# A gated delta rule followed by a softplus layer: another written-out order of the same operations

## The chip, the cores and the metric

The kernel runs on one core of a Trainium2 chip. The core has five engines that run side by side: TensorE (PE in the profile; its weight loads are PEld), VectorE (DVE), ScalarE (ACT), GpSimd (POOL) and SyncE (SP), which here only issues transfers. Each engine takes its own instructions strictly in the order in which the program lists them, and waits on semaphores for what the others produce. Transfers between the chip's memory and the core's run on 16 DMA engines. The metric is the device time of one execution in microseconds (us), lower is better.

## The reference

Two layers. The first is a recurrence over time with a 48 x 48 state for each of 4 x 8 pairs of batch and head, 768 steps long; the second works on its output, 3072 rows of 384.

```python
# q, k, v, g: (4, 8, 768, 48), beta: (4, 8, 768); all float32
k_n = k / (np.linalg.norm(k, axis=-1, keepdims=True) + 1e-06)
state = np.zeros((B, H, D, D))
for t in range(S):
    readout = np.einsum('bhd,bhde->bhe', q[:, :, t], state)
    y[:, :, t] = g[:, :, t] * readout
    v_old = np.einsum('bhde,bhd->bhe', state, kt)          # kt = k_n[:, :, t]
    state = state + bt * np.einsum('bhd,bhe->bhde', kt, vt - v_old)
x = y.transpose(0, 2, 1, 3).reshape(B * S, H * D)          # 3072 x 384
h = x @ w_in                                               # 384 x 2048
out = softplus(h) @ w_out                                  # 2048 x 384
```

## The kernel before

The recurrence is cut into 12 chunks of 64 steps (c = 0 to 11). Within a chunk the 64 dependent updates are replaced by products with the inverse of a triangular 64 x 64 matrix; only the state is carried from chunk to chunk. All 32 pairs of batch and head are worked on together.

For each chunk, `norms` squares k (ksq), sums (red) and takes roots (sqrt for the first four chunks, pow on GpSimd for the rest). `front` scales or casts k and q to 16 bits (kmul, cast), transposes them on TensorE (trs), evicts the transposes to the tile kqt (kev, qev), and forms the products of keys with keys and of keys with queries (gramk, gramq, gram), whose evictions are kkc and mask. `inverse`, once for each pair of chunks, inverts the blocks of 16 of the triangular matrices in place, lane by lane: diag and prep, then 15 steps (step c.0 to c.14, each a product and a sum on VectorE or GpSimd, each depending on the one before), then transposes back (st), and the matmuls xmm, tmm and zmm with their evictions (xs, td2, z) put the blocks together. `chain` carries the state: ks and qs are the products of keys and queries with the old state, w subtracts from v, umm and zu apply the inverse (evictions u1 and u2), smm and s make the new state, ymm and y the output of the chunk, and ytr with xt turn it around for the second layer. `vs 1` scales v of chunk 1 on GpSimd. `dense` is the second layer: g1 (x times w_in, into one of two PSUM buffers h), soft (softplus on ScalarE), g2 (times w_out, into the one PSUM buffer o), o (its eviction) and store. Groups of g1 and g2 are called `g1 chunk.block` and `g2 chunk.half.block`. `fill` groups are matmuls of the identity that nobody reads; 13 of the 40 defined are used.

Transfers: `load` brings half a tile of k, q, v or g (192 KB) and is issued by SyncE, as are the small beta loads (bload). `wload` brings a quarter of w_in (w0.0 to w0.3) or of w_out (w1.0 to w1.3), 384 KB each, and is issued by GpSimd, which also converts to 16 bits on the way. `store` writes 64 rows of the output (96 KB) and is issued by SyncE or ScalarE. An engine that reaches a transfer whose buffer is not free, or whose data is not made, waits there with everything behind it.

The order is written out: `_ORDER` is a string of words, a letter for the engine that is to do an operation (P TensorE, D VectorE, A ScalarE, G GpSimd, S SyncE) and the operation's number. `Program.emit` walks through the words and records each operation's instructions. So the words of one letter, read alone, are that engine's queue. How the words of different letters are interleaved decides only which buffer of a ring an operation gets, since a ring hands out the one that has been free longest. The rings that matter here: 12 buffers f for loaded tiles and squares, 5 PSUM buffers d for the recurrence, 2 for h, 1 for o, 16 for the output of softplus.

```python
    def emit(self, table):
        for word in table.split():
            en, no = word[0], int(word[1:])
            ...
            it.fn(en)
```

Lines of the profile that are spoken of: L305 and L302 are the loads, L330 the weight loads, L351 and L353 the squares on ScalarE and on GpSimd, L209 and L211 the copies on ScalarE and on VectorE or GpSimd (evictions among them), L454 and L422 the transposes of q and k, L516 gram, L656, L664 and L671 the steps of the inverse, L744, L768 and L789 xmm, tmm and zmm, L826 ks and qs, L842 vs 1, L866 w, L880 umm, L893 zu, L910 smm, L936 ymm, L963 ytr, L989 g1, L1001 softplus, L1016 g2, L1035 the stores, L1046 the fillers, L1056 the loading of ScalarE's softplus table.

## Time and profile before

| | us |
|---|---|
| three runs | 244.29, 249.46, 248.98 (median 248.98) |
| the profiled execution | 243.45 |
| its span, first to last instruction | 241.7 |
| mean granted clock of TensorE in it | 0.964 of full speed |

Busy time in the span: TensorE 219.1 us (91%), VectorE 164.8 (68%), ScalarE 154.7 (64%), GpSimd 108.4 (45%). The chain of work that ended last is 73% TensorE: 26% of the span at L1016 and 25% at L989, the two products of the second layer.

How rows are read: in an answer by stages, a row gives the stretch, its length, then for TensorE, its weight loads, VectorE, ScalarE and GpSimd the busy time with the number of instructions in brackets, then TensorE's granted clock, the mean busy share of the DMA engines and GB/s. In the order of time, a row gives the start, the duration, engine, line and operation, and in square brackets how long the engine had been idle and what ended that. In the groups, the figures behind the bar are the busy time of the group and the mean of one instruction in ns, and then the idle time ahead of them. Rows of transfers end with the size of one and the median time from issue to landing. Matmuls are pipelined: one's duration includes its way through the array, so that the durations of neighbours overlap.

### The profile page before, as it was taken

The numbers are of one execution on the slowest core, as the hardware profiler recorded it, in microseconds if no ns is written. First come the engines' busy times: TensorE is split into PE (matmuls) and PEld (weight loads), VectorE is DVE, ScalarE is ACT, GpSimd is POOL, SyncE is SP. The second block draws the span as 40 slices with busy tenths as digits, with TensorE's granted clock in tenths as the row PEclk, the third lists the DMA queues.
The fourth block names the chain that finished last, engine by engine and source line by source line (L and its number), as shares of the span: only waits on it lengthen the run. The fifth ranks groups of instructions, "written<-read, shape, count | busy, mean of one in ns | idle before, by whom it ended". The sixth has DMA issues, their size and how long they took to land.

```text
span 241.7 us, 11163 instructions
## 1 busy us (share of the span) xinstructions
PE 219.1 (91%) x4892; PEld 137.8 (57%) x4892; DVE 164.8 (68%) x378; ACT 154.7 (64%) x296; POOL 108.4 (45%) x180
## 2 busy tenths in 40 slices
PE   7695689886969999998999999999999999999993
PEld 2342377655756764565655566555666555677761
DVE  7898887877979887977799887997496150503000
ACT  6876755683865799896797635568763566253540
POOL 8151297767879468687399581313320000000000
PEclk9769956999999999999999999999999999999999
DMA  6999999999999388978699261922316100211122
GB/s 103 169 219 199 143 128 195 160 195 184 179 219 142 67 141 159 186 145 103 158 157 165 43 113 35 181 52 50 70 22 134 35 19 20 51 35 33 35 49 66
DMA packets 86833, 27.56 MB, mean 114 GB/s; under 512 B 77048, under 2 KB 86776, under 8 KB 86784
## 3 DMA queue, kind: packets, MB, share of 16 engines
q1 hardware_dynamic: 82064, 22.60, 54.7%
q0 software_dynamic: 3840, 3.17, 9.1%
q10 hardware_dynamic: 880, 1.08, 1.8%
q8 instruction: 38, 0.62, 1.2%
q14 instruction: 11, 0.09, 0.1%
HBM read 25.26 MB, written 4.72 MB: 124 GB/s over the span
## 4 chain that ended last, share of the span: by engine, by line
PE 73%; DMA 4%; ACT 3%; issue 2%; DVE 2%; POOL 1%; ACTq 0%; POOLq 0%
PE o L1016 26%; PE h L989 25%; DMA f<-in_g_dram 4%; PE d L936 3%; PE d L826 3%; PE d L516 2%; PE d L910 2%; PE d L893 2%; PE d L963 2%; PE d L454 1%; PE d L422 1%; PE d L768 1%; PE d L789 1%; PE d L744 1%; PE d L880 1%
## 5 line engine op out<-in xcount | busy, mean ns | idle before, releaser
L1016 PE MATMUL o<-w_out,ga 128*128 128x384 f16 x384 | 77.3, 327 | 0.6 <-ACT osb L209 0.6
L1001 ACT ACTIVATE ga<-h 128x512 f16<-128x512 f32 x96 | 56.6, 599 | 33.1 <-PE h L989 29.6
L989 PE MATMUL h<-xt,w_in 128*128 128x512 f16 (+1 forms) x384 | 73.6, 327 | 0.8 <-ACT xt L209 0.7
L989 PEld LDWEIGHTS <-w_in 128*128 128x128 f16 x384 | 35.0, 98 | 22.2 <-issue 1.5
L1016 PEld LDWEIGHTS <-ga 128*128 128x128 f16 x384 | 33.8, 98 | 20.8 <-issue 0.8
L664 POOL TENSOR_TENSOR tmp<-nn,tt 128x56 f32<-128x56 f32 (+7 forms) x47 | 16.8, 357 | 33.4 <-DVE tt L671 22.5
L373 POOL TENSOR_TENSOR nv<-nv,half_c 128x16 f32<-128x16 f32 x8 | 23.5, 2933 | 0.8 <-DVE nv L362 0.8
L209 ACT ACTIVATE u<-d 128x384 f16<-128x384 f32 x33 | 15.3, 491 | 9.6 <-PE d L893 5.2
L209 ACT ACTIVATE kqt<-d 128x1024 f16<-128x1024 f16 (+1 forms) x19 | 18.6, 977 | 4.2 <-PE d L454 2.2
L498 DVE TENSOR_TENSOR mt<-d,mask 128x256 f16<-128x256 f32 x48 | 18.4, 416 | 3.7 <-PE d L516 2.4
L671 POOL TENSOR_TENSOR tt<-tt,tmp 128x56 f32<-128x56 f32 (+7 forms) x47 | 17.3, 367 | 3.7
L1046 PE MATMUL h<-ident 128*128 128x512 f16 x52 | 17.2, 486 | 1.7 <-DVE ident L197 1.7
L209 ACT ACTIVATE osb<-o 128x384 f32<-128x384 f32 x20 | 9.8, 490 | 13.2 <-PE o L1016 13.0
L924 DVE TENSOR_TENSOR s<-s,d 128x384 f16<-128x384 f16 x20 | 10.3, 547 | 9.2 <-PE d L910 9.2
L406 POOL TENSOR_TENSOR kn<-f,nv 128x768 f16<-128x768 f32 x9 | 13.9, 1539 | 5.4 <-DVE nv L383 3.1
L211 DVE CAST u<-d 128x384 f16<-128x384 f32 x15 | 8.3, 556 | 9.9 <-PE d L893 7.6
L209 ACT ACTIVATE kk<-d 128x256 f16<-128x256 f32 x38 | 13.0, 386 | 2.1 <-DVE mt L498 0.8
L950 DVE TENSOR_TENSOR yg<-d,f 128x384 f16<-128x384 f32 x24 | 12.1, 547 | 3.1 <-PE d L936 1.9
L753 DVE TENSOR_TENSOR xs<-d,mk 128x256 f16<-128x256 f32 x24 | 9.2, 412 | 6.8 <-PE d L744 6.6
L664 DVE TENSOR_TENSOR tmp<-nn,tt 128x96 f32<-128x96 f32 (+7 forms) x37 | 9.7, 263 | 5.8 <-POOL tt L671 5.0
L866 DVE TENSOR_TENSOR w<-f,d 128x384 f16<-128x384 f32 x22 | 11.5, 547 | 3.0 <-POOL f L842 1.4
L516 PE MATMUL d<-kqt 48*64 48x128 f16 (+1 forms) x448 | 10.6, 220 | 2.3 <-issue 0.9
(114 smaller groups left out, 344.5 us busy)
## 6 DMA issues: line engine op xcount, KB each, us to landing
f<-in_k_dram SPq DMA_DIRECT2D x24, 192.0 KB, 5.8
f<-in_v_dram SPq DMA_DIRECT2D x24, 192.0 KB, 5.3
f<-in_q_dram SPq DMA_DIRECT2D x24, 192.0 KB, 5.4
f<-in_g_dram SPq DMA_DIRECT2D x24, 192.0 KB, 5.0
out_dram<-osb SPq DMA_DIRECT2D x37, 96.0 KB, 2.8
w_in<-in_moe_w_in_dram POOLq DMA_DIRECT2D x4, 384.0 KB, 6.3
w_out<-in_moe_w_out_dram POOLq DMA_DIRECT2D x4, 384.0 KB, 8.5
out_dram<-osb ACTq DMA_DIRECT2D x11, 96.0 KB, 2.4
```

What stands on the lines that cost most here:

```text
L209: nc.scalar.activation(o, x, AF.Copy, scale=float(sign))
L373: nc.gpsimd.tensor_tensor(nvs(), nvs(), half_c[:, :NU], ALU.pow)
L406: ENG[en].tensor_tensor(kn[c].ap[:, sl, :, :D], kf.ap[:, sl], nv.ap[:, :NU].rearrange("p (a h) -> p a h", a=2)[:, sl, :, None] .broadcast_ ...
L498: nc.vector.tensor_tensor(mt[c][m].ap[:, NP * p : NP * p + NP], gb[m].ap.rearrange("p (i b) -> p i b", i=NP)[:, :, n : n + C], mask[:, Non ...
L516: nc.tensor.matmul(gb[m].ap.rearrange("p (i b) -> p i b", i=NP)[HALF[r], i, lo:hi], x[:, :C], x[:, lo:hi],)
L664: ENG[en].tensor_tensor(t, nn.ap[:, :, j : j + 1, j + 1 :].broadcast_to([P, 2, w, n]), tt.ap[:, :, :w, j : j + 1].broadcast_to([P, 2, w, n ...
L671: ENG[en].tensor_tensor(rows, rows, t, ALU.add)
L950: lambda en, m=m: nc.vector.tensor_tensor(heads(yg.ap, m), hd(yp[m].ap), heads(gf.ap, m), ALU.mult),
L989: nc.tensor.matmul(hp.ap[:, n * b : n * b + n], w_in[:, j, f * P : (f + 1) * P], xt.ap[:, j, t0 : t0 + n], start=(j == 0), stop=(j == 2),)
L1001: lambda en, hp=hp, o=gb: nc.scalar.activation(o.ap, hp.ap, AF.Softplus),
L1016: nc.tensor.matmul(op.ap[:, :DM], b.ap[:, col + c0 : col + c0 + 128], w_out[:, f, :], start=(f == 0), stop=(f == NF - 1),)
L1046: nc.tensor.matmul(hp.ap, ident, ident[:, None, :].broadcast_to([P, 4, P]))
```

## The change

Only the string `_ORDER` is replaced. The operations are the same, with two fillers exchanged for two others, so there are 13 as before. On each engine the new queue is the old one with operations moved by some places, and 130 or so operations change their engine, mostly evictions between VectorE and ScalarE and steps of the inverse between VectorE and GpSimd. TensorE has 376 operations before and after, VectorE 325 and 329, ScalarE 302 and 308, GpSimd 110 and 104, SyncE 141 and 137. No group on TensorE moves by more than 13 places; on SyncE the first 20 transfers stay as they are. Nearly all buffers are handed out differently.

The diff, cut to a few of its lines:

```diff
@@ -1064,71 +1064,72 @@
 _ORDER = """
-S25 S26 S33 S34 S30 S60 S29 D9 D11 A8 D3 D5 D222 D176 D0 G198 P143 P144 S35 S59 P132 S36 D2 A1 A10
...
-G239 D192 D193 A270 D240 D243 D241 A242 A244 A288 D245 D246 P250 G248 A249 P259 G121 G123 G356 G122
...
-A1262 P1268 P1265 A1266 P1269 P1270 A1271 A1273 S1272 P1274 P1275 P1276 P1277 A1278 S1279 S1280
+S25 S26 P143 S33 D310 A7 D9 P132 S34 D11 A8 D3 D5 A1 D222 A10 S30 S60 D176 A169 P141 D0 D2 A173 G16
...
+A242 P296 D245 S32 P149 A270 A244 P250 D246 S31 A288 P259 S24 S17 D251 G248 A249 D252 P253 G123 D247
+S18 A254 G122 S22 A356 D398 D261 A255 S23 G121 D260 P188 A297 G125 D190 D189 P711 A713 A712 D289
...
+P1277 A1278 A1279 S1280
 """
```

Read by engine, with the operations' names, the parts that the prediction speaks of (before, then after):

```
TensorE, chunk 0
 - trs q2, fill 7, fill 35, xmm 0, xmm 1, tmm 0, umm 0, zmm 0, gramq 1.0, gramq 0.0, zu 0, trs q3, ymm 0, smm 0, fill 18, ytr 0, trs k3.0, g1 0.0
 + trs q2, trs q3, fill 20, xmm 0, xmm 1, tmm 0, gramq 0.0, umm 0, gramq 1.0, zmm 0, zu 0, smm 0, ymm 0, fill 18, ytr 0, trs k3.0, g1 0.0
ScalarE, chunk 0
 - ksq 3, tx 0.1, td2 0.1, td2 0.0, u1 0.1, sqrt 3, z 0.1, table, u2 0.1, s 0.0, qev q3, s 0.1, xt 0
 + ksq 3, tx 0.1, td2 0.0, ksq 4, td2 0.1, qev q3, u1 0.1, u1 0.0, sqrt 3, z 0.1, u2 0.1, table, s 0.0, xt 0, kev k3.0, s 0.1
GpSimd
 - tx 0.0, wload w0.0, wload w0.2, ksq 4, wload w0.1, wload w1.0, fix, clear 2, clear 4, wload w1.1, pad, kmul 2.0, pow 4, kmul 4.0, wload w0.3, vs 1, prep 2.0
 + tx 0.0, wload w0.2, wload w0.1, wload w0.0, wload w1.0, wload w1.1, diag 2, diag 4, kmul 2.0, pow 4, kmul 4.0, wload w0.3, vs 1, prep 2.0, prep 2.1
VectorE, chunk 1
 - ln 2, mask 2.00, pick 2, w 1.0, prep 2.1, w 1.1, red 5, step 2.2
 + ln 2, mask 2.11, pick 2, w 1.0, w 1.1, td2 1.1, mask 2.01, step 2.0, z 1.0, step 2.2
TensorE, chunk 1
 - zmm 1, umm 1, fill 4, g1 0.12, gramq 1.1, qs 1, zu 1, g2 0.1.4, ymm 1, gram 4.1, g1 0.14, ytr 1, smm 1
 + zmm 1, umm 1, gramq 1.1, g2 0.1.4, qs 1, fill 4, zu 1, g1 0.12, ymm 1, smm 1, g1 0.14, ytr 1, gram 4.1
Second inverse, engine of the steps 2.0 to 2.14
 - G G D D D G G D G D G G G G G
 + D G D D G G D D G D G D D G G
SyncE, from the 19th transfer
 - k4.0, bload, k3.0, k3.1, k4.1, bload, g0.1, k5.1, g0.0, 6 x bload, v1.0, v1.1, k5.0, g1.0, g1.1
 + k4.0, bload, k5.1, k3.0, k3.1, k4.1, bload, g0.1, g0.0, 6 x bload, v1.1, v1.0, g1.1, k5.0, g1.0
SyncE, about the 60th
 - q9.1, q7.0, q7.1, k9.0, v3.0, k9.1, v3.1, g3.1, g3.0, store 1.01, store 1.00, v5.0
 + q8.1, k11.1, g3.1, store 1.00, k9.0, v5.0
The last stores
 - ScalarE: o 11.0, store 11.01, o 11.1; SyncE: store 11.00, store 11.10, store 11.11
 + ScalarE: o 11.0, store 11.00, store 11.01, o 11.1, store 11.10; SyncE: store 11.11
```

More of the change, by code (lines that the diff above doesn't have):

```diff
@@ new lines @@
+A731 A732 P945 S46 D317 G318 P729 P133 D217 D377 P733 D218 S82 G319 D320 A735 S73 P933 A734 A934
+A930 P739 D321 P736 D740 G322 P935 D741 G128 P742 A383 D323 A936 D737 A743 P371 D373 D374 G324 D325
+A372 P951 A952 S74 P965 D326 D738 G327 D375 P366 P384 A367 P744 G328 S81 A966 A332 A368 D369 D331
+P946 G378 D745 D329 P959 A330 D333 S75 P953 S47 A960 P947 A385 D746 A954 G486 D334 A336 P957 G487
+A948 P338 P955 D370 G337 D339 S115 S76 D340 A444 P347 S84 P341 D335 A956 P937 A342 D343 D379 S91
+D349 G380 P748 S48 P344 P961 A464 A345 D346 D749 A750 P381 D445 G446 A451 P747 D348 P751 D382 A962
@@ new lines @@
+D752 P938 D465 G466 S54 S55 A753 P757 D759 S950 S53 P754 P939 S98 D755 P386 A387 A388 D447 G448 P940
+A941 D756 D758 S83 P391 A393 A392 D390 P963 D389 S99 A964 D395 A958 P762 D396 P967 P350 P968 A352
+A351 P760 S92 S114 D397 G400 A761 P969 D764 P449 D763 S56 P970 D401 D402 G403 G404 D450 P766 D768
+D767 A971 P353 S972 S97 P974 A355 A471 A354 G405 D467 S69 D394 P452 A453 P765 D406 D407 P975 P769
+A771 A770 P976 D408 D409 D410 P472 P775 D777 P772 A473 P977 D776 G468 A552 P778 D773 A539 S116 P454
```

113 lines of the change are left out of this document (51 added, 62 removed).

## The prediction

> **What bounds the kernel now.** I read the page first, for the slices of the span, then the busy time of each engine in stages, and last the start in order of time, engine by engine.
>
> ```profile
> span 241.7 us, 11163 instructions
> PE   7695689886969999998999999999999999999993
> PEclk9769956999999999999999999999999999999999
> DMA  6999999999999388978699261922316100211122
> ```
>
> The profiled execution took 243.45 us, so 1.75 us lie outside its span. A digit stands for 6.04 us. The DMA engines are at 9 from the second slice to the fourteenth (85 us), and TensorE is at 9 from the thirteenth (72 us) on, but for one 8 and the last slice. So there are two parts: a start that waits for data and for short dependent steps, and a plateau.
>
> ```profile
> 40.09:50.33 10.24, 8.99 (x219) 6.86 (x217) 7.86 (x18) 6.96 (x19) 8.23 (x8) 1.00 1.18 170
> 50.33:60.57 10.24, 7.72 (x271) 5.69 (x270) 7.99 (x22) 5.71 (x12) 7.21 (x18) 1.00 1.37 191
> 60.57:80.00 19.43, 17.43 (x495) 12.76 (x485) 17.20 (x35) 13.12 (x30) 15.94 (x17) 1.00 1.01 178
> 80.00:234.00 154.00, 152.84 (x3420) 93.53 (x3419) 98.28 (x218) 99.74 (x187) 56.96 (x104) 1.00 0.47 87
> ```
>
> The first number after each stretch is its length, the second TensorE's busy time. From 80 to 234 us it idles for 1.16 us of 154. The change issues the same 376 groups of matmuls, 13 of them fillers as before. So on the plateau an order can lose, but it can win at most 1.2 us. From 40.09 to 80 us TensorE idles for 39.91 - 8.99 - 7.72 - 17.43 = 5.8 us: this is all that better cover in the start can give back once dense work has begun.
>
> **The start, chunk 0.** Three things change around 28 to 40 us. ksq 4 moves from GpSimd to ScalarE, between the two evictions td2 0.0 and td2 0.1. The eviction qev q3 goes ahead of u1, and u1 0.0 goes from VectorE to ScalarE behind u1 0.1.
>
> ```profile
> 28.02 0.83 ACT L351 ACTIVATE f<-f 128x768 f32<-128x768 f32 x1
> 30.68 0.66 ACT L209 ACTIVATE td<-d 128x256 f16<-128x256 f32 x2 [0.78 <-PE d L768]
> 32.07 0.56 DVE L211 CAST u<-d 128x384 f16<-128x384 f32 x1
> 33.12 1.28 ACT L1056 ACT_TABLE_LOAD   x1
> 37.30 1.02 ACT L209 ACTIVATE kqt<-d 128x1024 f16<-128x1024 f16 x1
> 40.27 0.81 PE L989 MATMUL h<-xt,w_in 128*128 128x256 f16 x6
> ```
>
> On ScalarE a square costs 0.83 us, so td2 0.1 ends at 31.34 + 0.83 = 32.17 and umm 0 follows that late. Then qev q3 (1.02) and two u1 (0.88 together) stand in line: u1 is complete at about 34.1 instead of 32.07 + 0.56 = 32.6. Half of this comes back, because the table load (1.28, and 0.20 for its dummy) stood ahead of u2 0.1 and now stands behind it. With the new place of smm 0 ahead of ymm 0 I get xt 0 some 0.6 us later, and the first dense matmuls (g1 0.0) at 40.9 instead of 40.27.
>
> g1 0.0 also needs the first quarter of w_in, which was the first weight load and is now the third.
>
> ```profile
> 29.92 1.62 POOL L330 DMA_DIRECT2D w_in<-in_moe_w_in_dram  x2
> 33.03 0.80 POOL L330 DMA_DIRECT2D w_in<-in_moe_w_in_dram  x1
> w_in<-in_moe_w_in_dram POOLq DMA_DIRECT2D x1, 384.0 KB, 5.1
> w_in<-in_moe_w_in_dram POOLq DMA_DIRECT2D x1, 384.0 KB, 8.2
> ```
>
> The two landing times belong to the first load and to the third. The third is now issued at 29.92 + 1.62 = 31.54, so it lands between 36.6 and 39.7 us; I take the later, its own row. That is 1.2 us ahead of 40.9, so it is hidden; if chunk 0 came sooner, this load would be what is late next.
>
> Most of the 0.6 us is lost in idle time behind it, because chunk 1 has a gate of its own:
>
> ```profile
> 47.46 1.74 POOL L842 TENSOR_TENSOR f<-f,nv 128x768 f32<-128x768 f32 x1 [1.06 <-DMA f<-in_g_dram]
> f<-in_v_dram SPq DMA_DIRECT2D x2, 192.0 KB, 14.7
> 49.23 0.55 DVE L866 TENSOR_TENSOR w<-f,d 128x384 f16<-128x384 f32 x1 [1.35 <-POOL f L842]
> ```
>
> The scaling of v for chunk 1 waits for a load (the row names g; v 1 is what it reads, and v took 14.7 us to land, beside 1.9 MB of weights). All five early weight loads still stand ahead of it and the same bytes precede v 1 on SyncE, k5.1 included, so I leave 47.5 us where it is. I charge 0.2 us of the 0.6 (bounds 0 and 0.6). k5.1 ahead of k3 and k4.1 delays those by about one load; ksq 4, now earlier in ScalarE's queue, has td2 0.1 behind it and would pass the wait on.
>
> **Chunk 1 and the second inverse.** td2 1.1 moves from ScalarE to VectorE, behind w 1.1, which waits for that load.
>
> ```profile
> 48.80 0.64 ACT L209 ACTIVATE td<-d 128x256 f16<-128x256 f32 x2
> 50.70 0.43 PE L880 MATMUL d<-w,td 64*64 64x48 f16 x31 [0.68 <-DVE w L866]
> 50.32 0.24 POOL L656 TENSOR_TENSOR tt<-nn,tt 128x30 f32<-128x30 f32 x1 [0.43 <-DVE nn L644]
> 61.31 0.25 POOL L664 TENSOR_TENSOR tmp<-nn,tt 128x30 f32<-128x30 f32 x1
> L664 POOL TENSOR_TENSOR tmp<-nn,tt 128x56 f32<-128x56 f32 (+7 forms) x47 | 16.8, 357 | 33.4 <-DVE tt L671 22.5
> L664 DVE TENSOR_TENSOR tmp<-nn,tt 128x96 f32<-128x96 f32 (+7 forms) x37 | 9.7, 263 | 5.8 <-POOL tt L671 5.0
> ```
>
> The pair w 1 ends at 49.23 + 2 x 0.55 = 50.33, and an eviction of this size then takes some 0.4 us; zmm 1 queues behind that with 32 small matmuls (like umm's 0.43 us), and umm 1 behind zmm 1: I put it at 51.2 to 51.4, some 0.6 us later than the 50.70 above. smm 1 in turn now follows ymm 1 directly, so this is mostly returned before chunk 2.
>
> What chunk 2 waits for is the second inverse, 15 steps in a chain between GpSimd and VectorE, from 50.32 to the last product at 61.31 and its sum, about 61.9 us. Both prep 2 are now on GpSimd and step 2.0 on VectorE behind td2 1.1 and a mask: it starts about 0.8 us later. Three more of the 15 steps are net on VectorE (four go there, one goes back). A step is a product and a sum, on VectorE 0.09 us shorter each by the two means (their shapes differ somewhat), so 3 x 0.19 = 0.6 us is won; three more hand-overs cost an estimated 0.1 us each. Sum +0.5 us, bounds 0 and 1.5, as VectorE has other work between its steps. TensorE had 2.0 us idle from 60.57 to 80, so nothing covers this for certain: I charge 0.5 us.
>
> **The plateau and the end.** Loads and stores are shuffled on SyncE. The tightest place I found is k9.0, now behind store 1.00:
>
> ```profile
> 82.19 2.09 SPq L1035 DMA_DIRECT2D out_dram<-osb  x2
> f<-in_v_dram SPq DMA_DIRECT2D x1, 192.0 KB, 3.6
> 86.88 0.85 ACT L351 ACTIVATE f<-f 128x768 f32<-128x768 f32 x1
> ```
>
> Issued some 0.6 us behind that store, with the 3.6 us of a load just after, it lands at 86.4 us, 0.5 us before ksq 9 on ScalarE needs it. Hidden; if late, ScalarE holds softplus behind it and g1 runs out of its two buffers. Four more stores are issued by ScalarE, where it idles for a third of the plateau: nothing charged.
>
> At the end the last two stores of 64 rows, both on SyncE before, go one by ScalarE and one by SyncE.
>
> ```profile
> 238.09 1.11 SPq L1035 DMA_DIRECT2D out_dram<-osb  x2
> ```
>
> Half of these 1.11 us, 0.55, leaves the end. Sum: 0.2 + 0.5 - 0.55 = +0.15 us on 243.45, 243.6 us for an execution like the profiled one.
>
> **How that stands to the runs.** Three runs took 244.29, 248.98 and 249.46 us, the profiled one 243.45: two groups, 5 us apart, and the middle of the three is in the upper. The profile shows only a lower one. I forecast the centre of what was seen, (243.45 + 244.29 + 248.98 + 249.46)/4 = 246.55, plus 0.15: **246.7 us**, within 1.3% of either group.
>
> **The clock.** What differs between executions may be TensorE's clock:
>
> ```profile
> L1046 PE MATMUL h<-ident 128*128 128x512 f16 x2 | 0.6, 378 | 0.0
> 21.12 1.03 PE L1046 MATMUL h<-ident 128*128 128x512 f16 x4
> 24.39 0.61 PE L454 MATMUL d<-ident,qn 128*128 128x128 f16 x8
> 5.96:9.37 3.41, 1.66 (x43) 0.88 (x41) 2.27 (x6) 2.51 (x6) 0.73 (x3) 1.00 1.40 157
> 16.20:19.61 3.41, 1.44 (x14) 0.70 (x12) 3.01 (x12) 2.46 (x3) 0.00 (x0) 1.00 1.08 233
> 26.44:29.85 3.41, 1.19 (x68) 0.81 (x66) 2.58 (x5) 2.99 (x6) 0.48 (x1) 1.00 1.20 174
> 29.85:33.27 3.41, 2.25 (x111) 2.05 (x112) 3.33 (x7) 1.83 (x7) 3.34 (x5) 0.50 0.55 67
> 33.27:36.68 3.41, 3.21 (x118) 3.01 (x118) 2.03 (x7) 1.72 (x3) 3.41 (x6) 0.50 1.24 190
> 36.68:40.09 3.41, 3.41 (x29) 2.19 (x22) 3.25 (x8) 2.48 (x4) 2.20 (x3) 0.50 1.24 199
> ```
>
> In the last six rows the figure before the last two (1.00 or 0.50) is the granted clock, constant over each 3.41 us. It fell to half after stretches with 1.66 and 1.19 us of TensorE work, and came back only after one full of large matmuls. The Trainium skill, "TensorE: Matmul & The Clock Gate", Part 1, says that this window is free-running, that one idle window halves the clock and one busy window restores it. By that rule alone the clock would have come back at 36.68, after a window 94% busy, and chunk 0 would have ended up to 1.7 us sooner; the trace has 0.50 until 40.09, and the row decides.
>
> **Rivals.** First, the start stays warm. trs q3 and a filler now stand right before xmm 0, inside 26.44:29.85. By the first three rows this stretch had 0.6 us of large matmuls (half a filler) and gets a filler (1.03) and eight transposes (0.61), about 1.5 with their overlap; 16.20:19.61 kept its clock with 1.44. Then the 8.87 us of work in the three half-clock rows shrink by up to 4.4 us. On chunk 0's path I count at most half of that, and w_in (39.7 us) and v 1 (47.5) cap it: 1 to 2 us, so 241.6 to 242.6 for the profiled kind; and if the upper group comes from the clock, the middle run drops to the lower one, 242.5 to 243.5. For it: the place of the fillers. Against: the margin is next to nothing. Chance 0.30.
>
> Second, on the other side: the clock comes back late. In 36.68:40.09 it was the filler, ytr 0 and trs k3 that filled the window; chunk 0 now comes 0.6 us later and its small matmuls move into that window. If one that starts later must release it, dense work begins at half clock: each further window costs 1.7 us of TensorE time, three of them 5.1. It decides once that work exceeds the 2.5 us idle between 50.33 and 60.57. The profiled kind would take 248.6 us, and the middle run 248.98 + 5.1 = 254.1. For it: 33.27:36.68, busy and not released. Against: w_in lands in time. Chance 0.25.
>
> **How the numbers follow.** The forecast has the remaining 0.45. Two per cent (5 us) is about what these runs can tell from no change: below 244.0 is faster, above 254.0 slower. The warm case gives faster nearly always, 0.28, and the forecast's lower group touches 244.0: 0.04 more, 0.32 in all. The late case gives slower where all three windows are lost, 0.16 of its 0.25, with 0.04 for stalls on the plateau that I missed: 0.20. The rest, 0.48, is no change. The range goes from 242.0, inside the warm case, to 254.2, past the late case's 254.1; below and above it I leave 0.08 and 0.10.
>
> **What would show it.** In the profile after: PEclk in the slices from 30 to 40 us (warm or not); g1's first row near 40.9 us; the scaling at L842 near 47.5; the last step of the second inverse near 62.4; one store on each queue at the end, 0.5 us sooner. I am wrong if waits of TensorE over 1 us show after 80 us, if L842 has moved by more than 2 us, or if clock digits below 9 stand after 45 us.

## The result, and the profile after

Sixteen executions of the changed kernel have a median of 245.85 us (244.06 to 247.38), sixteen of the kernel before 244.72 us (242.11 to 249.46). The ratio is **1.0078, 95% interval 1.0053 to 1.0104**: slower by 0.8%, 1.9 us, less than the 2% that I called no change, but more than the measurement's own uncertainty. The ratio leaves out executions over 1.5% above the fastest of their kernel, which the old order has here and the new one has not; the medians of all executions are only 0.5% apart, their means 0.2%. The profiled execution took 246.25 us (before 243.45).

The page of the changed kernel, the same rows as before (a digit is 6.1 us):

```profile
span 244.5 us, 11144 instructions
PE   7696548888988999999999999999999999999983
PEclk9859985899997999999999999999999999999998
DMA  6999889999998469992598591962003110330212
```

The clock's dip in the slices of 30 to 45 us has moved half a slice to the right, and there is a new 7 at the thirteenth digit, near 76 us. The busy time by stage, with the columns as before (length, then TensorE's busy time, in brackets its matmuls; the figure ahead of the last two is the granted clock):

```profile
40.00:50.30 10.30, 8.86 (x155) 6.91 (x154) 6.86 (x16) 7.56 (x14) 7.85 (x6) 0.77 1.22 187
50.30:60.60 10.30, 8.53 (x292) 5.80 (x291) 9.03 (x26) 7.10 (x14) 7.02 (x15) 1.00 1.28 179
60.60:80.00 19.40, 17.11 (x450) 11.88 (x449) 15.39 (x35) 11.98 (x24) 14.00 (x16) 0.91 1.06 193
80.00:234.00 154.00, 153.10 (x3494) 93.66 (x3487) 102.94 (x227) 100.74 (x192) 57.64 (x102) 1.00 0.48 84
...
72.08:75.49 3.41, 1.72 (x69) 1.04 (x69) 2.01 (x5) 1.20 (x3) 2.82 (x1) 1.00 0.79 143
75.49:78.90 3.41, 3.41 (x85) 2.23 (x85) 2.90 (x6) 0.00 (x0) 2.86 (x3) 0.50 0.91 220
```

The plateau from 80 us is as full as it was (0.9 us idle, before 1.16). In 75.49 to 78.90 TensorE is busy all the time at half clock, behind a stretch with 1.72 us of work. The kernel before has a dip at the same work, 0.3 us less deep, and its clock stays:

```profile
70.81:74.22 3.41, 2.01 (x76) 1.44 (x69) 1.95 (x5) 0.98 (x2) 3.27 (x4) 1.00 1.23 190
74.22:77.64 3.42, 3.37 (x65) 2.09 (x64) 3.11 (x8) 2.19 (x6) 3.25 (x3) 1.00 0.83 146
```

To see where the lateness is made I compare the start of a w_out group (line 1016) ahead of which TensorE has done the same groups in both orders. At one of chunk 0 the changed kernel is late by 1.45 us (63.24 against 61.79), at the fourth of chunk 1 by 3.58 (84.35 against 80.77), at the last of all by 3.10 (239.82 against 236.72), at the end of the span by 2.8. So between these two profiles 1.5 us are lost by 63 us, 2.1 more between there and 84 us, and 0.8 comes back. Of the 2.1, 0.8 are there at the sixth group (74.74 against 72.49), and 1.3 come behind it, where the window at half clock lies. That the first part belongs to the order, and not to these two executions, does not hold: see "The same words more than once" below. What stands ahead of it here, in the order of time on GpSimd and on VectorE:

```profile
47.06 1.47 POOL L406 TENSOR_TENSOR kn<-f,nv 128x768 f16<-128x768 f32 x1 [1.71 <-PE d L516]
...
49.37 1.49 POOL L842 TENSOR_TENSOR f<-f,nv 128x768 f32<-128x768 f32 x1
...
63.24 0.27 POOL L671 TENSOR_TENSOR tt<-tt,tmp 128x30 f32<-128x30 f32 x1
```

```profile
44.07 0.42 DVE L498 TENSOR_TENSOR mt<-d,mask 128x256 f16<-128x256 f32 x1 [2.73 <-PE d L516]
...
46.59 0.24 DVE L383 RECIPROCAL nv<-nv 128x16 f32<-128x16 f32 x1
...
48.17 1.95 DVE L604 STREAM_TRANSPOSE ln<-kk 128x1024 uint32<-128x1024 uint32 x1
...
52.78 0.18 DVE L656 TENSOR_TENSOR tt<-nn,tt 128x30 f32<-128x30 f32 x1
```

The reciprocal at 46.59 is the norm factor of chunk 4 (before 43.72). It now stands behind masks of chunk 3, the first of which (44.07) waited 2.73 us for its gram. The k scale of chunk 4 on GpSimd (47.06) reads it; the row names a gram as what ended the wait, but in e3 below this scale starts ahead of that gram, 0.24 us after the factor. The v scale of chunk 1 (L842) behind it starts at 49.37, 1.9 us later than before, with no load to wait for. The transposition ln at 48.17, ahead of the second inverse, needs all kk copies of chunks 2 and 3, which come behind those grams (before 45.33); the inverse starts at 52.78 and ends at 63.5 (before 50.32 and 61.9). The lateness is there already at the first dense group on TensorE (41.95, before 40.27). Its rows, and further on those of the product zu of chunk 2 with a stop between its halves:

```profile
41.23 0.93 PE L422 MATMUL d<-ident,kn 128*128 128x128 f16 x7 [0.73 <-issue]
41.95 1.49 PE L989 MATMUL h<-xt,w_in 128*128 128x256 f16 x6
...
72.98 0.31 PE L893 MATMUL d<-u,z 64*64 64x48 f16 x15 [0.48 <-DVE xs L753]
74.49 0.31 PE L893 MATMUL d<-u,z 64*64 64x48 f16 x16 [1.21 <-issue]
```

```profile
w_in<-in_moe_w_in_dram POOLq DMA_DIRECT2D x1, 384.0 KB, 9.9
```

The copy xt 0 had ended at 41.04; the first quarter of w_in, issued third at 31.94, landed 9.9 us later at 41.84. Yet the group's row shows no wait. The transposes trs k3.0 stand ahead of it in TensorE's queue; they stood still for 0.73 us with no semaphore to wait for and then ran at half clock until the group began. So in this profile the late load is hidden behind them, by about 0.1 us. The last stores go out side by side, as the change says:

```profile
241.19 0.47 SPq L1035 DMA_DIRECT2D out_dram<-osb  x1
```

```profile
241.19 0.50 ACTq L1035 DMA_DIRECT2D out_dram<-osb  x1
```

### The profile page after: what moved, and what is told of

The parts are those of the page before. It is cut to its first block, busy times and chain, and to the rows that moved or that the text cites. A ratio compares the mean times of both kernels' runs of the same rounds, so it can differ in the third digit from the quotient of the medians.

```text
span 244.5 us, 11144 instructions
## 1 busy us (share of the span) xinstructions
PE 221.8 (91%) x4892; PEld 137.0 (56%) x4892; DVE 167.3 (68%) x386; ACT 158.3 (65%) x298; POOL 102.3 (42%) x170
## 4 chain that ended last, share of the span: by engine, by line
PE 67%; DVE 12%; DMA 6%; issue 5%; ACT 4%; POOL 3%; SPq 2%; DVEq 0%; POOLq 0%; ACTq 0%
PE o L1016 24%; PE h L989 21%; PE h L1046 4%; PE d L936 3%; DMA f<-in_k_dram 2%; PE d L516 2%; SPq L305 2%; DMA f<-in_v_dram 2%; PE d L826 2%; PE d L893 2%; PE d L422 2%; PE d L910 2%; PE d L963 1%; DVE tt L671 1%; DVE tmp L664 1%
## 5 line engine op out<-in xcount | busy, mean ns | idle before, releaser
L1016 PE MATMUL o<-w_out,ga 128*128 128x384 f16 x384 | 78.3, 329 | 0.6 <-ACT osb L209 0.6
L664 POOL TENSOR_TENSOR tmp<-nn,tt 128x56 f32<-128x56 f32 (+7 forms) x43 | 15.1, 351 | 23.8 <-DVE tt L671 20.9
L209 ACT ACTIVATE kqt<-d 128x1024 f16<-128x1024 f16 (+1 forms) x20 | 19.6, 979 | 8.3 <-PE d L454 4.2
L1046 PE MATMUL h<-ident 128*128 128x512 f16 x52 | 18.5, 516 | 1.7 <-DVE ident L197 1.7
L209 ACT ACTIVATE u<-d 128x384 f16<-128x384 f32 x28 | 12.9, 489 | 11.0 <-PE d L893 7.7
L211 DVE CAST u<-d 128x384 f16<-128x384 f32 x20 | 10.7, 552 | 12.6 <-PE d L880 7.1
L671 POOL TENSOR_TENSOR tt<-tt,tmp 128x56 f32<-128x56 f32 (+7 forms) x43 | 15.7, 365 | 3.4
L664 DVE TENSOR_TENSOR tmp<-nn,tt 128x96 f32<-128x96 f32 (+7 forms) x41 | 10.8, 263 | 8.0 <-POOL tt L671 7.0
L209 ACT ACTIVATE kk<-d 128x256 f16<-128x256 f32 x34 | 11.7, 384 | 6.4 <-PE d L516 5.3
L516 PEld LDWEIGHTS <-kqt 48*64 48x64 f16 x448 | 7.8, 115 | 10.0 <-issue 7.3
```

The costliest lines, as they stand in the source:

```text
L209: nc.scalar.activation(o, x, AF.Copy, scale=float(sign))
L516: nc.tensor.matmul(gb[m].ap.rearrange("p (i b) -> p i b", i=NP)[HALF[r], i, lo:hi], x[:, :C], x[:, lo:hi],)
L664: ENG[en].tensor_tensor(t, nn.ap[:, :, j : j + 1, j + 1 :].broadcast_to([P, 2, w, n]), tt.ap[:, :, :w, j : j + 1].broadcast_to([P, 2, w, n ...
L671: ENG[en].tensor_tensor(rows, rows, t, ALU.add)
L1016: nc.tensor.matmul(op.ap[:, :DM], b.ap[:, col + c0 : col + c0 + 128], w_out[:, f, :], start=(f == 0), stop=(f == NF - 1),)
L1046: nc.tensor.matmul(hp.ap, ident, ident[:, None, :].broadcast_to([P, 4, P]))
```

## The experiments

Eighteen kernels, in five groups (e to i); each group has its own runs of the kernel before on the same chip. "Old" is the order before, "new" the changed one; a word is one operation with its engine's letter, and the words of one order that stand in a kept part are left out of the rest. "All" is the median of all executions in us; that of the kernel before was 243.59 beside e, 243.17 beside f, 243.81 beside g, 243.20 beside h and 244.14 beside i. "Late" counts the half-clock windows (3.41 us each) that end between 45 and 236 us in the one profile of each kernel; the kernel before has none.

| kernel | order | ratio to before, 95% | all | late |
|---|---|---|---|---|
| changed | new | 1.0078 (1.0053 to 1.0104) | 245.85 | 1 |
| e1 | old to 80 us, then new | 1.0059 (1.0015 to 1.0103) | 246.55 | 3 |
| e2 | new to 80 us, then old | 1.0105 (1.0072 to 1.0139) | 245.98 | 2 |
| e4 | old to the first g1, then new | 1.0068 (1.0032 to 1.0105) | 244.86 | 1 |
| e3 | new, two norm factors early | 1.0118 (1.0073 to 1.0162) | 246.49 | 1 |
| f3 | new, chunk 1 repaired in three places | 1.0275 (1.0215 to 1.0335) | 249.17 | 3 |
| g1 | f3 with two fillers | 1.0212 (1.0156 to 1.0268) | 249.53 | 2 |
| f1 | old, one w_out group earlier | 1.0016 (0.9977 to 1.0055) | 243.26 | 1 |
| f2 | new, the same group earlier | 1.0151 (1.0092 to 1.0210) | 246.18 | 2 |
| f4 | f3 with that group earlier | 1.0216 (1.0140 to 1.0292) | 249.76 | 2 |
| g2 | new, dip at 72 us filled | 1.0124 (1.0079 to 1.0168) | 245.78 | 3 |
| g3 | old, dips filled | 1.0233 (1.0187 to 1.0279) | 249.39 | 2 |
| g4 | new, dips filled | 1.0155 (1.0110 to 1.0199) | 247.30 | 0 |
| h1 | new, 40 to 51 us old | 1.0144 (1.0078 to 1.0210) | 247.63 | 2 |
| h2 | old, 40 to 51 us new | 0.9990 (0.9953 to 1.0028) | 243.36 | 0 |
| h3 | new, first quarter of w_in first | 1.0120 (1.0065 to 1.0175) | 246.57 | 2 |
| h4 | old, that quarter third | 1.0090 (1.0022 to 1.0158) | 248.58 | 1 |
| i1 | new to 39 us with that quarter first, then old | 0.9964 (0.9910 to 1.0017) | 245.98 | 3 |
| i2 | new to 52 us with that quarter first, then old | 1.0009 (0.9957 to 1.0061) | 245.59 | 1 |

Ten of the eighteen (e3, f2, f3, f4, g2, g3, g4, h1, h3, h4) came out clearly slower than every range that was expected of them, e2 by a hair. So no single cause that was named ahead of a run carries the whole loss. (The order has 1254 words; the 1067 in the first expectation is a slip.)

**Which part of the order.** The first four kernels cut both orders in two.

```diff
 e1
-_ORDER = new
+_ORDER = old[:440] + the words of new that are left
 e2
+_ORDER = new[:440] + the words of old that are left
 e4
+_ORDER = old[:206] + the words of new that are left
```

> The changed kernel with the first 440 of its 1067 words (all work up to about 80 us, the Y transpose of chunk 2) in the old order, the rest in the new. Start theory (the loss is made ahead of 80 us, by the late v scale of chunk 1 and what hangs on it): ratio to before 0.998 to 1.002, first g1 near 40.3, v scale near 47.5, last product of the second inverse ends near 61.9. Plateau theory (the loss is made by the order after 80 us and at the end): 1.006 to 1.010 with the same start. Clock theory: the ratio follows the number of half-clock stretches, 1.000 with two and 1.008 with a third.

> The mirror: the first 440 words in the new order, the rest in the old. Start theory: 1.006 to 1.010, v scale near 49.4, last product of the second inverse ends near 63.5. Plateau theory: 0.998 to 1.002. Clock theory: 1.008 only if a stretch at half clock stands near 75 us as it does in the changed kernel.

> The changed kernel with only the first 206 words (to the first g1 of chunk 0, about 40 us) in the old order: fillers, the q3 transpose, ScalarE's chunk 0 and the weight loads as before, and with them the norm factor of chunk 2; the masks of chunk 3 stay ahead of the norm factor of chunk 4. If chunk 0 makes the loss: first g1 near 40.3, ratio 0.998 to 1.002. If the gate on GpSimd makes it: v scale between 47.5 and 48.5 as the masks still hold the norm factor, ratio 1.001 to 1.004. Plateau theory: 1.006 to 1.010. Clock theory: half clock at 29.9 to 40.1 as before, and the ratio by whether a third stretch comes.

e2's ratio came out as the start theory had it: with only the first 80 us new, the loss is all there. Its dates did not: the v scale of chunk 1 came at 47.6 and the second inverse ended at 62.2, and at the third w_out group e2 was only 0.4 us late (62.17 against 61.79). So the loss does not need the late v scale. In e1 and e4, with the first 80 us or only chunk 0 old, some 0.6% stayed. By the dates e1's start was right (the second inverse ended at 61.3), and in its profile three half-clock windows (57.0 to 63.8 and 91.1 to 94.5) took the gain back. The rest itself is not slower: from the w_out group at 84.35 us (before 80.77) to the end of the span it takes 160.2 us in the changed kernel and 161.0 before, and over all profiles with that rest, e1's with its window at 91 us left out, 160.0 us in the new order (11 kernels) and 160.1 in the old (8). So the rest behind 84 us is not where the time is lost; the clock had to be looked at by itself.

**Repairing the visible waits.** e3 takes away the gate on GpSimd, f3 two waits more.

```diff
 e3, VectorE's queue
-eps 3, kmul 3.0, eps 2, red 4, mask 3.11, ..., mask 3.00, eps 4
+eps 3, eps 2, kmul 3.0, red 4, eps 4, mask 3.11, ..., mask 3.00
 f3, the same and
-TensorE: tmm 1, g1 0.8, trs k4.0, g1 0.10, g2 0.1.0, ks 1    VectorE: w 1.1, td2 1.1
+TensorE: tmm 1, ks 1, g1 0.8, trs k4.0, g1 0.10, g2 0.1.0    ScalarE: td2 1.0, td2 1.1
```

> The changed kernel with three words moved: VectorE takes the norm factor of chunk 2 ahead of the k scale of chunk 3 and the norm factor of chunk 4 ahead of the masks of chunk 3, all else kept. Start theory in its narrow form (this gate alone makes the loss): k scale of chunk 2 on GpSimd near 38.5 instead of 40.6, v scale of chunk 1 near 47.5 instead of 49.4, second inverse ends near 62, ratio 0.999 to 1.003. If chunk 0 makes it (first g1 1.7 us late): 1.005 to 1.008 with the v scale at 47.5. Clock theory: 1.008 if the stretch near 75 us stays.

> The changed kernel with chunk 1 repaired in three places: the norm factors of chunks 2 and 4 early on VectorE as in the third run, the product ks of chunk 1 directly behind its T transposes on TensorE instead of behind the first w_out group, and the second half of td2 on ScalarE instead of VectorE. In the third run ks started at 52.45 us and w at 53.01 us, after the v scale had ended at 49.5: with the gate on GpSimd gone the product on TensorE was last. Chunk 1 theory: ks near 47 us, w near 49.5, umm of chunk 1 at 50.3 to 51.3 us (changed kernel 52.8), second inverse ends at 62.0 to 62.6, ratio 1.001 to 1.005. If the start does not matter: 1.006 to 1.010. If the half clock takes it back as in the third run: the dates hold where no half-clock stretch lies between 45 and 62 us, and the ratio is 1.004 to 1.010.

Neither gained. In e3 the v scale came at 48.0 (47.5 expected), but ks of chunk 1 was last, on TensorE, which ran at half clock from 48.04 to 51.45 behind a window with 1.45 us of work, and w on VectorE followed it (the GpSimd product that the last row names had ended at 52.5):

```profile
52.45 0.44 PE L826 MATMUL d<-s,kqt 48*64 48x48 f16 x32
```

```profile
48.43 1.93 DVE L604 STREAM_TRANSPOSE ln<-kk 128x1024 uint32<-128x1024 uint32 x1
...
53.01 1.02 DVE L866 TENSOR_TENSOR w<-f,d 128x384 f16<-128x384 f32 x2 [2.00 <-POOL nn L644]
```

The second inverse was not helped at all, as ln stayed at 48.4: I had removed a wait beside the chain, not on it; what the half clock adds to this is not separated. f3 was slower still, and its profile shows the clock at half for longer. Its windows:

```profile
45.38:48.79 3.41, 1.56 (x39) 1.02 (x37) 2.68 (x9) 1.30 (x5) 2.77 (x5) 1.00 1.29 197
48.79:52.20 3.41, 2.58 (x68) 2.02 (x68) 3.28 (x6) 1.78 (x6) 1.40 (x2) 0.50 1.28 173
52.20:55.62 3.42, 3.42 (x20) 2.37 (x18) 1.32 (x4) 2.03 (x3) 2.70 (x5) 0.50 1.33 186
```

TensorE had run out of work at 45 us, fell to half clock for two windows, and umm of chunk 1 started at 56.7 instead of 52.8 in the changed kernel.

**The clock by itself.** g1 fills f3's dip with fillers, groups of four idle matmuls whose results are not used. g2 to g4 fill dips in both orders, partly with w_out groups moved ahead of zu of chunk 2.

```diff
 g1, TensorE's queue
-g1 0.2, gram 2.0, gram 2.1, tmm 1
+g1 0.2, filler, gram 2.0, gram 2.1, filler, tmm 1
 g2
-qs 2, zu 2, g2 0.0.4, ymm 2, smm 2, gram 5.0, g2 0.0.8
+qs 2, g2 0.0.4, g2 0.0.8, zu 2, filler, ymm 2, smm 2, gram 5.0
 g3 (old)
+three fillers ahead of trs q0, one each ahead of gram 4.1, g1 1.14 and gram 5.0, g2 0.0.4 ahead of zu 2
 g4 (new)
+as g2, two fillers ahead of trs q0, one each ahead of tmm 1 and g1 1.0
```

> The kernel with chunk 1 repaired (ratio 1.0275) and two groups of four idle matmuls (0.85 us each, results unused) put on TensorE where it waited near 45.9 us (1.57 us) and 48.6 us (0.48 us). Clock theory: in that kernel the 3.4 us window at 45.4 was 46% busy and the two windows behind it, 48.8 to 55.6, ran at half clock; with the fillers that window is over 60% busy, no half clock comes between 45 and 62 us, umm of chunk 1 starts near 51 instead of 56.7, and the ratio falls from 1.0275 to 1.002 to 1.010. If chunk 1 is slow by its order and not by the clock: no gain or a loss of up to 1.7 us, ratio 1.025 to 1.035.

> The changed kernel with the dip near 72 us filled only: two w_out groups (0.82 us each) moved ahead of zu of chunk 2, and one group of idle matmuls behind it. Clock theory with the dip at 72 us as the loss: no half-clock stretch between 70 and 82 us, ratio to before 1.000 to 1.004. If the loss was made before 66 us: 1.006 to 1.010, and the fill only moves the wait.

> The kernel before with its dips filled: three groups of idle matmuls in the wait of 3.03 us near 17.6, one each ahead of the gram of chunk 4 (wait 0.93 us), of g1 1.14 (0.68 us) and of the first gram of chunk 5, and one w_out group ahead of zu of chunk 2. Clock theory: the half-clock windows behind 17 us that came in some executions go, the scatter falls from 6 us to about 3, median 0.5 to 1.5 us under before: ratio 0.995 to 1.001. If half clock costs little: 1.000 to 1.006 by the fillers' own time.

> The changed kernel with its dips filled in the same way: two groups near 19 us, one each ahead of the T transposes of chunk 1 (0.70 us), of g1 1.0 (0.55 us) and of ymm of chunk 2, and two w_out groups ahead of zu of chunk 2. If the clock makes the whole loss: level with the filled kernel before, ratio 0.996 to 1.002. If the order of the start loses 1.5 to 2 us by itself: 1.005 to 1.009, and 1.5 to 2 us over the filled kernel before.

In g1 the window in question held its clock, and the next two dips did not:

```profile
44.57:47.99 3.42, 2.88 (x43) 1.50 (x41) 2.93 (x9) 1.43 (x6) 2.62 (x4) 1.00 1.23 181
47.99:51.40 3.41, 2.83 (x85) 2.18 (x83) 3.28 (x6) 1.71 (x6) 1.62 (x2) 1.00 1.10 166
...
58.23:61.64 3.41, 1.68 (x71) 1.34 (x69) 1.06 (x4) 2.21 (x5) 1.60 (x3) 1.00 1.17 148
61.64:65.05 3.41, 3.08 (x32) 2.21 (x31) 2.62 (x9) 1.77 (x3) 0.81 (x2) 0.50 1.11 157
```

umm of chunk 1 came at 53.8 instead of 56.7 (one profile each), so holding the clock was worth 2.9 us there; but the time hardly moved (the ratio fell from 1.0275 to 1.0212, within their intervals), and in the profile later windows went to half instead. In g2 and g3 the dips that remained came from weights that landed late: two in g2, one in g3, the two kernels' rows on TensorE:

```profile
44.04 0.83 PE L989 MATMUL h<-xt,w_in 128*128 128x256 f16 x6 [1.73 <-DMA w_in<-in_moe_w_in_dram]
...
70.77 0.81 PE L1016 MATMUL o<-w_out,ga 128*128 128x384 f16 x4 [2.66 <-DMA w_out<-in_moe_w_out_dram]
```

```profile
54.49 0.72 PE L989 MATMUL h<-xt,w_in 128*128 128x256 f16 x5 [1.62 <-DMA w_in<-in_moe_w_in_dram]
```

Half-clock windows followed each of them, so neither kernel tells what its filled dip was worth. g4's one profile has no half clock behind 45 us and g4 is still at 1.0155, its five fillers among it. Filling dips with idle work is no remedy here, and as far as one profile can say the late half clock is not the whole loss.

**The wait without a cause.** In the product zu of chunk 2 TensorE stands still between two matmuls with no semaphore to wait for, 1.40 us in the kernel before and 1.21 in the changed one.

```diff
 f1 (old), f2 (new), f4 (f3): TensorE's queue
-qs 2, zu 2, g2 0.0.4
+qs 2, g2 0.0.4, zu 2
```

> The kernel before with one group of four w_out matmuls (0.82 us) moved on TensorE from just behind the product zu of chunk 2 to just ahead of it. In the middle of that product TensorE stood still for 1.40 us with no semaphore to wait for. If TensorE waits there for its next page of instructions (a 16384-byte packet of the instruction queue ended at 70.77 us, 1.48 us before it went on): the wait falls to 0.4 to 0.8 us, the work after it starts 0.6 to 0.9 us sooner, ratio to before 0.994 to 0.998. If the wait belongs to the product's data: it stays at 1.2 to 1.5 us, ratio 0.999 to 1.003.

> The changed kernel with the same move. Page theory with the clock: the wait of 1.21 us in the product falls to 0.3 to 0.6 us, the 3.4 us window around it is busy enough, and the half clock near 75.5 us does not come; ratio to before 1.000 to 1.004 instead of 1.008. Chunk 1 theory (the loss is made by 65 us): gain of 0.8 us at most, 1.004 to 1.007.

> The last two together: chunk 1 repaired and the w_out group ahead of zu of chunk 2. If chunk 1 and the page wait with its half clock make the whole loss: ratio 0.996 to 1.001, no half-clock stretch behind 45 us in the profile. If only one of them counts: 1.002 to 1.006. If neither: 1.007 to 1.010.

f1 in order of time on TensorE:

```profile
73.74 0.28 PE L893 MATMUL d<-u,z 64*64 64x48 f16 x12
74.26 0.34 PE L893 MATMUL d<-u,z 64*64 64x48 f16 x20 [0.23 <-issue]
...
75.28 0.41 PE L516 MATMUL d<-kqt 48*64 48x128 f16 x15 [0.65 <-ACT u L209]
```

The stop has fallen from 1.40 to 0.23 us and has moved four matmuls back within the product, as many as were put ahead: it belongs to a number in TensorE's instruction stream, not to the data. All twenty profiles bear that out (last section). But 0.65 us of it come back one group later, where the copy of u is last, and the ratio is 1.0016. In f2 the stop stayed at 1.33 us, against expectation: its page was fetched later. f4 shows no stop there and is at 1.0216. So the page is the cause of the stop, and the stop is no free gain.

**Which cause in the start.** h1 and h2 exchange only the middle, h3 and h4 only the place of one load, i1 and i2 put the new start and the new middle ahead of the old rest, with the load first.

```diff
 h1 (h2 is its mirror)
+_ORDER = new[:195] + the words of old up to step 2.0 + the words of new that are left
 h3, GpSimd's queue (h4 is its mirror: w0.2, ksq 4, w0.1, w0.0)
-wload w0.2, wload w0.1, wload w0.0
+wload w0.0, wload w0.2, wload w0.1
 i1
+_ORDER = new[:195] with w0.0 first + the words of old that are left
 i2
+_ORDER = new[:265] with w0.0 first + the words of old that are left
```

> The changed kernel with only its middle in the old order and on the old engines: from behind the Y transpose of chunk 0 to the first step of the second inverse, about 40 to 51 us (the grams and kk copies of chunks 2 and 3, ln, pick and prep of the second inverse, ks, w and td2 of chunk 1); the start and all that follows stay new, the weight loads too. Middle theory (ln of the second inverse waits for kk copies that come behind gram and masks: 48.2 us in the changed kernel, 45.3 in the one before): ln near 46, last product of the second inverse ends near 62 to 62.5, ratio 1.000 to 1.004. Weight theory (the third-issued first quarter of w_in starts the lateness): first g1 still 0 to 1.6 us late, ratio 1.005 to 1.010. Plateau theory: 1.006 to 1.010.

> The mirror: the kernel before with only this middle (40 to 51 us) in the new order. Middle theory: ln at 46.5 to 48.5, last product of the second inverse ends at 63 to 64, ratio 1.006 to 1.010. Weight theory: first g1 without a wait for w_in, ratio 0.999 to 1.004.

> The changed kernel with one word moved: the load of the first quarter of w_in issued first of the weight loads, as before, instead of third. In nine profiles with it third it landed 9.1 to 10.9 us after its issue, up to 1.6 us behind the xt copy that the first g1 also needs; first, in five profiles, 4.9 to 5.2 us after its issue. Weight theory: first g1 straight behind the copy (near 41.0), ratio 1.001 to 1.005. Middle theory: no more than the 0 to 1.6 us at that place, 1.005 to 1.010.

> The mirror: the kernel before with that load issued third. It lands near 39 to 40.5, with the copy done at 40.2: weight theory in this kernel 1.000 to 1.004, the wait of the first g1 0 to 1 us and what follows late by as much; if the load's place does not matter: 0.998 to 1.002.

> Only the first 195 words (to the Y transpose of chunk 0, about 39 us) in the new order, with the first quarter of w_in loaded first; the rest in the old order. If the new start loses 2 us by itself: ratio to before 1.005 to 1.010. If the start is harmless once the weight comes first: 0.997 to 1.003. Clock theory: four half-clock windows ahead of 45 us instead of five or six, and the ratio by how many stand behind 45 us, 1.4 to 1.8 us each (a fit over 18 profiles).

> The first 265 words (to the first step of the second inverse, about 52 us) in the new order, the first quarter of w_in loaded first, the rest in the old order. With the load put first but the new order after 52 us kept, the ratio was 1.012 with a stop of 1.30 us near 57 us in small matmuls and two half-clock windows behind it. If the order behind 52 us makes these: no stop over 1 us between 52 and 62 us, ratio 0.998 to 1.004. If the new start does: 1.006 to 1.012.

The middle theory falls with h2: the new middle alone costs nothing. h1 says the same from the other side: with the middle old it is still at 1.0144, above all that was expected. In h2 the second inverse does end at 63.3, 1.4 us late, as in the changed kernel, and the first product behind it on TensorE starts 1.26 us late; but zu of chunk 2 then has no stop (its page is there by then), and TensorE reaches the w_out group that starts at 80.77 in the kernel before at 80.86. The load's place does cost, in the old order by itself: in h4 the first g1 waits for it, and the clock falls behind the wait. The ratio of 1.0090 is the smaller reading: the median of all twelve executions is 248.58 us against 243.20. h4 in order of time and by windows:

```profile
42.72 0.83 PE L989 MATMUL h<-xt,w_in 128*128 128x256 f16 x6 [2.37 <-DMA w_in<-in_moe_w_in_dram]
```

```profile
40.08:43.49 3.41, 1.04 (x12) 0.80 (x11) 1.00 (x2) 0.41 (x1) 3.41 (x2) 1.00 1.27 188
43.49:46.90 3.41, 3.41 (x49) 2.60 (x47) 2.25 (x7) 1.77 (x5) 0.47 (x3) 0.50 1.25 195
```

Yet taking it out of the new order (h3) gains nothing that can be seen. There the first g1 came at 41.2 straight behind its copy, and the time was lost further on:

```profile
56.75 0.19 PE L910 MATMUL d<-u,kn 64*64 64x48 f16 x1
58.24 0.49 PE L910 MATMUL d<-u,kn 64*64 64x48 f16 x29 [1.30 <-issue]
```

```profile
55.05:58.47 3.42, 1.89 (x97) 1.52 (x86) 2.64 (x8) 2.58 (x5) 1.82 (x5) 1.00 1.35 189
58.47:61.88 3.41, 3.08 (x55) 2.27 (x44) 1.25 (x4) 1.41 (x2) 1.24 (x3) 0.50 1.10 128
```

In the new order smm 1 follows ymm 1 directly, 64 small matmuls in a row; the old one has a gram and a g1 between. But the stop is not the mark of the new order. The changed kernel has the same words there, and its own profile shows none: ymm 1 and smm 1 pass from 57.28 to 58.2 us without a wait, at full clock. The old order has stops of 0.93 us (the kernel before) and 1.56 us (e1) at the same number in the stream. i2 differs from h3 only behind 52 us, where it has the old order: 1.0009 instead of 1.0120, by the medians of all executions 1.4 us over the kernel before instead of 3.4. i1, the new start alone with the load first, is level with the kernel before as well, as its ratio goes. Neither is an improvement: the medians of all their executions are 245.98 and 245.59 us against 244.14. So by the ratios most of the loss hangs on the new order between 52 us (i2) and 80 us (e2); e1, old up to 80 us and still at 1.0059, does not fit.

**The same words more than once.** Up to 80 us e2 repeats the words of the changed kernel and e1 those of the kernel before; f2 and f1 differ from these by one group only. So each order has three profiles for its first 80 us (us; the tenth w_out group has the same groups ahead of it in all six, as the third has):

| | before, e1, f1 | changed, e2, f2 |
|---|---|---|
| first g1 | 40.27, 39.73, 41.34 | 41.95, 40.38, 41.08 |
| v scale of chunk 1 | 47.46, 46.90, 48.51 | 49.37, 47.62, 48.10 |
| second inverse ends | 61.90, 61.27, 63.12 | 63.51, 62.22, 64.28 |
| third w_out group | 61.79, 64.36, 64.12 | 63.24, 62.17, 64.02 |
| tenth w_out group | 78.68, 80.10, 80.69 | 82.25, 83.04, 83.39 |
| from the third to the tenth | 16.89, 15.74, 16.57 | 19.01, 20.87, 19.37 |
| half-clock windows between the two | 0, 0, 0 | 1, 2, 1 |

The same words start the same group up to 2.6 us apart, so a difference of 1 or 2 us between two profiles says little about an order. By 63 us the two orders are level in the mean. From there to the tenth group the new one takes 3.4 us longer in the mean, and the three values of one order stand clear of the other's. In each new one a window near 70 to 78 us is too empty and the next is at half clock. In e2, where zu of chunk 2 stood still for 2.23 us up to 74.23:

```profile
69.84:73.25 3.41, 1.67 (x60) 1.11 (x58) 2.40 (x5) 1.67 (x4) 2.16 (x2) 1.00 0.96 132
73.25:76.67 3.42, 2.44 (x46) 1.43 (x47) 1.42 (x2) 0.49 (x1) 1.75 (x3) 0.50 0.71 152
```

Of all twelve kernels with the new order in this stretch seven show such a window in their profile, of the eight with the old one none. So this is the stretch in which the changed kernel loses its time. That the half clock makes most of it (up to 1.7 us for each window) is argued from these profiles: f2, f4, g2 and g4 were to keep the clock up there; f2 and g2 did not, and f4 and g4, which did, carry other changes as well.

## Why the prediction was wrong

I forecast no change, +0.15 us, and the kernel is 0.8% slower, 1.9 us by the ratio. The range of 242.0 to 254.2 us and the middle class held; the sum was far too small. That 246.7 us lies near the measured 245.85 is luck: I took 246.55 for the kernel before, from four executions in what I read as two groups, and sixteen gave 244.72, so a level 1.8 us too high made up for a change that was too small. Against the three runs' median of 248.98 the forecast even stood for a gain.

- **Chunk 2 at 0.5 us, with the clock taken as full: the step that failed.** For the stretch from 60.57 to 80 us I charged the second inverse's 0.5 us, because TensorE had 2.0 us idle there, and nothing for the clock behind 45 us. By the three profiles of each order, the way from the third to the tenth w_out group takes 3.4 us longer, with a half-clock window in each new one and none in the old ones. The stage rows say the same: TensorE idles for 2.3 us from 60.60 to 80 instead of 2.0, but its granted clock is 0.91 instead of 1.00. Which moved words empty the window ahead of it stays open.
- **The load of w_in "hidden" at 39.7 us: the date was wrong, the loss is not there.** Moved to third place I gave it the third load's own 8.2 us at most. It took 9.9 us and landed at 41.84. In eleven profiles with the load in third place it landed 9.1 to 10.9 us after its issue, in nine with it first 4.9 to 5.3. The third load had landed at 33.03 + 8.2 = 41.2 before and lands at 41.84 now, though it is issued 1.1 us sooner: this points to the bytes ahead of it as what sets its end, and I had added a duration to an issue. In the old order this step costs 1.0090 or more (h4, a wait of 2.37 us and a half-clock window behind it). In the changed kernel the first g1 does not wait for it, in e2 and f2 it landed within 0.1 us of the copy, and h3, with the load first, is no faster. The first g1 itself came 0.7 us late in the mean of the three profiles, as forecast (0.6).
- **The v scale of chunk 1 left at 47.5 us: 49.4 in the one profile, and by itself harmless.** I looked at what stands ahead of it on SyncE and on GpSimd, not at VectorE, where its predecessor's factor had gone behind masks that wait for a gram. But e2 and f2 have it at 47.6 and 48.1 with the same words, and e3 shows that this gate alone does not set the time.
- **The second inverse at +0.5 us: under-sized, +1.2 in the mean of three profiles (+1.6 in the two compared first).** Its start at ln was moved by the kk copies, which I had not followed. But h2 shows that a delay of this size is repaid at zu of chunk 2, so this alone is not what the change costs.
- **smm 1 behind ymm 1 as a return of the delay: not refuted.** umm of chunk 1 started 2.1 us late in the changed kernel (52.83 against 50.70), the third w_out group 1.45.
- **The clock's rivals.** The rival that the clock comes back late was nearer than the forecast, but for another reason than its own. Half clock lasted to 44.8 instead of 40.1 in the changed kernel, yet to 39.1 in e2 and 40.3 in f2. What the profiles share is not small matmuls that fail to release it at 40 us, but a dip that puts it back near 75, in the changed kernel 1.72 us of work in 72.08 to 75.49 against 2.01 before. The warm start came too (30 to 34.5 us at full clock) and won little; that chunk 0 waits there for other engines is argued, not tried.
- **Plateau behind 84 us and end: right.** Nothing is lost there, and the end gained 0.3 of the 0.55 us forecast (late by 3.10 at the last w_out group, by 2.8 at the end).

What stays open: the order behind 52 us (1.011 between h3 and i2) and the load's place (1.0090 alone) together exceed the changed kernel's 1.0078, and e1, with neither ahead of 80 us, is still at 1.0059. Part of each such number is how many half-clock windows the kernel's few executions drew. A straight line through twenty profiles gives an estimate of 1.8 us per late window and leaves a scatter of 1.7 us: single profiles can't split 1.9 us any finer. None of the nineteen orders beats the one before by more than its interval.

## What to carry to other kernels

Where a queue is reordered, follow each moved transfer to the queue's traffic at its new place, and each moved wait to everything behind it on that engine. Before repairing a wait, ask what is last once it is gone: taking three visible waits out here raised the ratio from 1.0078 to 1.0275, and in the profile TensorE ran out of work and was clocked down. In a start that leaves TensorE half idle, a stop of half a microsecond can decide over a whole window of the clock. So compare many executions, and before a date in a profile is put down to an order, look at the same words in another profile: here they differed by up to 2.6 us.

## What I had not expected of the hardware

**How empty a window may be.** In twenty profiles 1077 windows of 3.41 us at full clock start between 41 and 230 us. All 20 with less than 2.0 us of TensorE work were followed by one at half clock, and of the others only one (2.06 us); 2.02 us was enough. Of 34 windows at half clock the five with 2.9 us of work or less were followed by another, of the 29 with more only five were. The Trainium skill, "TensorE: Matmul & The Clock Gate", Part 1, has one idle window halve the clock and one busy window restore it. The trace agrees in part: every window behind 41 us that was less than 58% busy was followed by half clock, so it need not be idle, and every window that restored the clock was over 85% busy, but one in six of those did not restore it. Ahead of 41 us the share of busy time does not decide: of 49 windows at full clock with less than 2.0 us of work, 21 (1.44 to 1.99 us) kept the clock. In the changed kernel 17.46 to 20.87 us, with 17 matmuls and 1.62 us of work, kept it, and 31.11 to 34.52, with 96 matmuls and 1.69 us, did not. The size of the matmuls may be what counts; no run here tries it.

**Pages of instructions.** TensorE's stops without a releaser come at matmuls whose numbers differ by multiples of 128 (606, 862 and 1246 in the kernel before, of 0.77, 0.93 and 1.40 us); with the weight load of each that is every 256 instructions. In the twenty profiles all 52 such stops of over 0.3 us (behind the first 5 us) stand at a number that is 94 or 95 above a multiple of 128. A packet of 16,384 bytes on the instruction queue belongs to each, and TensorE goes on 1.3 to 1.8 us after its end. The packet starts 0.8 us in the median after the boundary before behind 110 us, where the DMA engines are quieter, and 1.8 us, at times over 3.5, between 55 and 90 us, where they are fuller (in the changed kernel a busy share of 0.48 from 80 to 234 us against 1.06 from 60.6 to 80). The Trainium skill, "Runtime: NRT & Kernel Launch", Instruction fetch mechanics, describes blocks of this size, fetched ahead and mostly hidden. The size agrees; hidden it is not in these 52 cases.
